# Token-tile pairs of the MoE second layer as 2x2 blocks with seven products, and a new order of the steps

## The chip, the cores and the metric

The kernel runs on one core of one Trainium2 chip. The metric is the device time of one execution in microseconds (us), median of 3 runs. The engines are named as the profile names them: PE (TensorE matmul), PEld (its weight loads), DVE (VectorE), ACT (ScalarE), POOL (GpSimd), SP (the queue that issues the DMAs).

## The reference, cut to what matters

Three stages follow one another: a pooled attention that makes x (2304 tokens, 512 features), a mixture of 8 experts that all see all tokens, and a last two-layer network. The change is in the second of them:

```python
for e in range(E):                       # E = 8, F = 1024, D = 512
    h = np.maximum(x @ w1[e], 0.0)       # first layer
    ye = h @ w2[e]                       # second layer
    out += P[:, e:e + 1] * ye            # gate of each token and expert
```

## The kernel before

A **unit** `u` is 256 of the 8192 hidden columns (two blocks `f` of 128), so there are 32 units, four to an expert. Units 4 to 31 run in the loop that the change touches; each goes through four **slots** `b` = 0 to 3, one for each batch of 576 tokens. Every matrix is held as a high and a low part, and a product is three matmuls (`PASSES`: high by high, high by low, low by high).

In a slot the **first layer** (`mm1w`) is already done by blocks: seven products `m1` to `m7` of 288 columns each on three PSUM banks a, b and e (pool `h`, four banks), with running sums copied out by ACT (`snap`, L588) and added by DVE (`plus`, L591). ACT then writes the high part of `h` (L579) and DVE the low part (L580). PE's inputs for it, `zz`, are made from `zp` by `z_add` (POOL, L535) and `z_split` (ACT L542, POOL L543), one batch ahead. `zp` itself comes once in a unit: `z_heads` (PE, L506, takes all four banks of pool `y`), `z_out` (ACT L516, then a store by SP) and `z_home` (four loads by SP, L524).

The **second layer** is `tile2`: for a tile of 128 tokens six matmuls of 512 columns (L645) into a bank of pool `y`, which DVE multiplies with the gate and adds to `acc` (`put1`, L663). A unit has 18 tiles, in the slots 4, 5, 4 and 5; those of one slot are worked off in the slot after it, between the seven products (`slotw`).

Around this run `w1_split` (ACT L243, POOL L244) and `load_w2` (ACT L131, POOL L132), which split the weights of the next unit, and `conv_units`, the decoding of weights of the last stage, one DVE instruction to a slot from unit 9 on (L151 to L162).

The order of all instructions is written out by hand (`manual_schedule`): each engine executes its own in the order in which the code issues them, and waits where an operand or a buffer isn't ready.

Of the kernel before, what the change touches and what calls it, by code (L numbers as in the profile page):

```python
# [29 lines left out]
BLK = 384  # L30
# [10 lines left out]
W0 = UE  # L41


@with_exitstack
def tile_kernel(ctx: ExitStack, tc: tile.TileContext, qT, kT, vv, pb, w1c, w2c, wcat64, wg, sv, bv, out):
# [7 lines left out]
    far_p = pool("far", 4, space=bass.MemoryType.DRAM)  # L53
    banks = {}
# [78 lines left out]

    RAWS = [(v, half, f) for v in range(1, U2) for half in (1, 0) for f in range(UF)]
# [9 lines left out]

    def raw_ops(key, q):

        v, half, f = key
        lo, hi, m = raw_parts(raws[key], q)
        ex = wt_p[-1].tile([128, 256], U32, tag="ex", name="ex")
# [12 lines left out]
        yield lambda: V.scalar_tensor_tensor(out=m if v else plain(f)[:, o], in0=m, scalar=2.0 ** 20,  # L162
                                             in1=ex.bitcast(F32), op0=ALU.add, op1=ALU.mult)

# [398 lines left out]
    LEFT = {1: 0, 4: 1, 2: 2, 5: 3, 6: 4, 7: 5, 3: 6}  # L563
# [11 lines left out]
    def h_put(b, f, t, p_):  # L575
        s_ = p_[:, :HB]
        o = (b % 2) * S + t * HB
        hh, hl = (h[:, f, k, o:o + HB] for k in range(2))
        A.activation(out=hh, in_=s_, func=AF.Relu)  # L579
        V.scalar_tensor_tensor(out=hl, in0=s_, scalar=0.0, in1=hh.bitcast(F32), op0=ALU.max, op1=ALU.subtract)  # L580

    def mm1w(u, b):

        p, s_ = {}, {}

        def snap(n):
            s_[n] = wt_p[-1].tile([128, BLK], F32, tag=f"snap{n % 2}", name="snap")[:, :HB]
# [5 lines left out]
        def j1():  # L593
            p["a"], p["b"] = psa("h", "ps_a"), psa("h", "ps_b")
            product(1, u, b, p["a"], True)
            snap(1)
            product(2, u, b, p["b"], True)
            plus(1, "b", "b")
            h_put(b, 1, 0, p["b"])

        def j2():
            p["e"] = psa("h", "ps_e")
            product(6, u, b, p["a"])
            snap(2)
            product(7, u, b, p["e"], True)

        def j3():
            product(5, u, b, p["a"])
            snap(3)
            plus(3, "e", "b")  # L610
            h_put(b, 0, 1, p["b"])

        def j4():
            product(3, u, b, p["a"])
            h_put(b, 1, 1, p["a"])
            product(4, u, b, p["e"])
# [19 lines left out]
    def tile2(ws, h, hc, T, put):  # L636
# [10 lines left out]
        put(T, y, acc[:, T, :])  # L647
# [204 lines left out]
    def made(u, pr, q):  # L852
# [3 lines left out]
        return [lambda t=t: tile2(ws, *cols(t), pr * 9 + t, put1(u))  # L856
# [8 lines left out]

    def slotw(u, b, side):

        todo, jobs = ready[:], mm1w(u, b)
        ready[:] = made(u, b // 2, 2 * (b % 2)) + made(u, b // 2, 2 * (b % 2) + 1)
        for n in range(5):  # L870
            for q_, at_ in ((jobs, n + 0.5), (todo, n)):
                if q_:
                    q_.pop(0)()
                for s in side.get(at_, ()):
                    s()

# [35 lines left out]
    with tc.tile_pool(name="ppf", bufs=1) as ppf_p, tc.tile_pool(name="w1p", bufs=2) as w1_, ExitStack() as whole, ExitStack() as start:  # L912
# [163 lines left out]
        conv = {}  # L1076

        def w2_(u):
            if ("w2", u) not in conv:
                conv["w2", u] = load_w2(u)  # L1080
            next(conv["w2", u], None)

        units = conv_units()

        with tc.manual_schedule():
            first = {(0, 1): [(w2_, W0), (x_split, 0)],
                     (0, 2): [(x_split, 1), (x_add, 2)],
                     (0, 3): [(w2_, W0)],
                     (1, 0): [(z_half, W0, 0), (z_half, W0, 1), (x_split, 2)],
                     (1, 1): [(x_add, 3), (load_w1, W0 + 1)],  # L1090
# [5 lines left out]
            for u in range(W0, U1):  # L1096
                for b in range(B):
                    side, last = {n / 2: [] for n in range(10)}, u == U1 - 1
                    if b + 1 < B:
                        side[0].append((z_split, u, b + 1))  # L1100
                    if b + 2 < B:
                        side[3].append((z_add, u, b + 2))
                    if u == W0 and b == 0:
                        side[3].append((pp_split, ))
                    if u == W0 and b == 2:
                        side[1].append((x_split, 3))
                    if last and b < 2:
                        side[2].append((split_plain, b, 0))
                        side[4].append((split_plain, b, 1))
                    if not last:  # L1110
                        if b == 0:
                            side[0].append((w2_, u + 1))
                            side[1].append((w1_split, u + 1, 0))
                            side[2].append((w1_split, u + 1, 1))
                            side[4].append((w2_, u + 1))
                        if b == 1:
                            side[1.5] += [(z_heads, u + 1), (z_out, 0)]
                            side[1].append((z_out, 1))
                        if b == 2:
                            side[0].append((z_home, u + 1))  # L1120
                        if b == 3:
                            side[0].append((z_add, u + 1, 0))
                            side[2].append((z_split, u + 1, 0))
                            side[4].append((z_add, u + 1, 1))
                            if u + 2 < U1:
                                side[2].append((load_w1, u + 2))
                    if u > U1 // 4 and not last:
                        side[(2, 0, 2, 1)[b]].append((next, units, None))
                    if last and b > 2:
                        side[1] += [(low, ), (raw_load, *RAWS[1])]  # L1130
                        side[2].append((low, ))
                    if last and b > 1:
                        for c in range(NC):
                            side[1 + c].append((flip, b - 2, c))
                    slotw(u, b, {n: [lambda f=f, a=a: f(*a) for f, *a in fs] for n, fs in side.items()})
# [4 lines left out]
        sums.append(wt.tile([128, 512], F32, name="sums"))  # L1140
# [97 lines left out]
```

## Time and profile before

| | |
|---|---|
| median of 3 runs | 1702.03 us (1699.96 to 1704.18) |
| profiled execution, span | 1698.2 us |
| around the span, by the median | 3.8 us |
| PE / DVE / ACT / POOL busy | 99% / 67% / 51% / 52% |

The span runs from the first to the last instruction of the core in one profiled execution. The runs were timed without a profile, and no run's own time belongs to the profiled execution alone; the median less the span stands for what lies around it. Busy shares are averages over stages.

### The profile page before, as it was taken

The page shows a single profiled execution, that of the slowest core. Times are in us where ns is not written, and L with a number is a line of the kernel's source. Part 1 is how long each engine was busy: PE and PEld are TensorE (multiplying, and loading weights), DVE is VectorE, ACT ScalarE, POOL GpSimd, SP SyncE. Part 2 cuts the span into 40 slices and gives each one's busy share as a digit, 9 for nine tenths or more (in the row PEclk, how much of TensorE's full clock was granted, in tenths as well). Part 3 has the DMA queues.
Part 4 walks back from the last instruction along what each step waited for, and adds up shares of the span by engine and source line. Part 5 has one row for each costly group of instructions (what it writes and reads, how often), then busy time and mean ns, then how long its engine had stood idle before and what let it go on. Part 6 is the DMA issues. An engine that isn't in the chain of part 4 may idle for free.

```text
span 1698.2 us, 27249 instructions
## 1 busy us (share of the span) xinstructions
PE 1673.7 (99%) x10075; PEld 1449.8 (85%) x10075; DVE 1139.1 (67%) x2246; ACT 874.3 (51%) x1948; POOL 884.0 (52%) x1070
## 2 busy tenths in 40 slices
PE   6999999999999999999999999999999999999999
PEld 4678888888888888888888888888888999989998
DVE  5656656666666666667666667666667877777763
ACT  3543364454454444454544445445445666666664
POOL 0332375555554555655655555555552855555552
PEclk9999999999999999999999999999999999999999
DMA  9610013223232333322332342222310111111103
GB/s 266 170 26 21 18 48 101 77 75 88 75 98 77 101 97 90 87 75 75 95 93 78 99 109 75 75 75 75 100 38 13 38 40 43 44 38 49 48 16 112
DMA packets 60725, 128.13 MB, mean 75 GB/s; under 512 B 5808, under 2 KB 27312, under 8 KB 60592
## 3 DMA queue, kind: packets, MB, share of 16 engines
q1 hardware_dynamic: 60592, 126.39, 27.1%
q8 instruction: 79, 1.29, 0.3%
q14 instruction: 54, 0.44, 0.1%
HBM read 93.34 MB, written 33.03 MB: 74 GB/s over the span
## 4 chain that ended last, share of the span: by engine, by line
PE 96%; DVE 2%; ACT 1%; DMA 1%; issue 0%; SPq 0%; POOL 0%; ACTq 0%; DVEq 0%
PE ps L645 58%; PE ps_a L572 10%; PE ps L688 9%; PE ps_e L572 5%; PE ps L627 3%; PE ps_b L572 3%; PE ps_z L506 3%; PE ps_a L758 1%; DMA q__116<-qT 1%; PE ps_e L758 1%; PE ps_z L452 0%; PE ps_f L810 0%; PE ps_b L758 0%; PE ps_q L346 0%; PE ps_v L331 0%
## 5 line engine op out<-in xcount | busy, mean ns | idle before, releaser
L645 PE MATMUL ps<-w,h 128*128 128x512 f32 x4296 | 1088.4, 394 | 2.9 <-ACT h L579 1.2
L645 PEld LDWEIGHTS ps<-w,h 128*128 128x128 f32 x4296 | 774.5, 188 | 150.1 <-ACT stage L516 4.8
L663 DVE SCALAR_TENSOR_TENSOR acc<-ps,pm,acc 128x512 f32<-128x512 f32 x504 | 372.2, 744 | 167.9 <-PE ps L645 166.9
L543 POOL TENSOR_TENSOR zz<-zp,zz 128x384 fp32r<-128x384 f32 x112 | 115.7, 1033 | 248.2 <-ACT zz L542 137.3
L588 ACT COPY snap<-ps_a 128x288 f32<-128x288 f32 x336 | 134.3, 400 | 204.6 <-PE ps_a L572 203.0
L535 POOL TENSOR_TENSOR sums<-zp 128x128 f32<-128x128 f32 x224 | 105.0, 469 | 167.3 <-DMA zp<-far 163.0
L580 DVE SCALAR_TENSOR_TENSOR h<-ps_b,h 128x288 fp32r<-128x288 f32 x224 | 102.5, 458 | 106.7 <-ACT h L579 106.7
L579 ACT ACTIVATE h<-ps_b 128x288 fp32r<-128x288 f32 x224 | 92.2, 411 | 147.8 <-DVE ps_b L591 147.8
L543 POOL TENSOR_TENSOR zz<-sums,zz 128x512 fp32r<-128x512 f32 x112 | 145.1, 1296 | 0.0
L802 DVE TENSOR_TENSOR acc<-ps,acc 128x512 f32<-128x512 f32 x126 | 86.1, 687 | 82.2 <-PE ps L645 82.0
L572 PEld LDWEIGHTS ps_a<-xt,zz 128*128 128x128 f32 x672 | 113.3, 188 | 18.8 <-ACT snap L588 0.5
L572 PEld LDWEIGHTS ps_a<-xa,zz 128*128 128x128 f32 x672 | 113.1, 188 | 18.0
L680 POOL TENSOR_TENSOR h<-gt,h 128x384 fp32r<-128x384 f32 x64 | 65.9, 1029 | 120.0 <-ACT h L679 110.6
L572 PE MATMUL ps_a<-xt,zz 128*128 128x288 f32 x672 | 125.9, 296 | 0.1
L572 PE MATMUL ps_e<-xt,zz 128*128 128x288 f32 x672 | 125.7, 296 | 0.0
L572 PE MATMUL ps_a<-xa,zz 128*128 128x288 f32 x672 | 125.7, 296 | 0.0
L579 ACT ACTIVATE h<-ps_e 128x288 fp32r<-128x288 f32 x112 | 46.1, 411 | 140.1 <-DVE ps_e L591 140.1
L688 PE MATMUL ps<-xa,w 128*128 128x384 f32 x432 | 110.4, 336 | 0.0
L688 PE MATMUL ps<-xt,w 128*128 128x384 f32 x432 | 110.1, 335 | 0.0
L572 PEld LDWEIGHTS ps_e<-xt,zz 128*128 128x128 f32 x672 | 101.9, 188 | 0.0
L132 POOL TENSOR_TENSOR w<-raw,w 128x1024 fp32r<-128x1024 f32 x31 | 74.5, 2405 | 27.0 <-ACT w L131 26.5
L580 DVE SCALAR_TENSOR_TENSOR h<-ps_e,h 128x288 fp32r<-128x288 f32 x112 | 51.2, 458 | 53.0 <-ACT h L579 53.0
(263 smaller groups left out, 2394.8 us busy)
## 6 DMA issues: line engine op xcount, KB each, us to landing
far<-stage SPq DMA_DIRECT2D x54, 512.0 KB, 2.9
zp<-far SPq DMA_DIRECT2D x108, 256.0 KB, 4.9
raw<-w2c SPq DMA_DIRECT2D x32, 512.0 KB, 7.6
raw<-wcat SPq DMA_DIRECT2D x32, 512.0 KB, 3.8
acc<-kT SPq DMA_DIRECT2D x8, 576.0 KB, 9.4
out<-acc SPq DMA_DIRECT2D x18, 256.0 KB, 2.0
acc<-vv SPq DMA_DIRECT2D x5, 576.0 KB, 10.5
q__114<-qT SPq DMA_DIRECT2D x1, 576.0 KB, 11.6
```

The costliest lines, as they stand in the source:

```text
L132: eng.tensor_tensor(out=w[:, 1, :], in0=r, in1=w[:, 0, :].bitcast(F32), op=ALU.subtract)
L535: G.tensor_tensor(out=sums[:, n], in0=x_, in1=y_, op=op)
L543: G.tensor_tensor(out=zz[:, 1, o], in0=s_, in1=zz[:, 0, o].bitcast(F32), op=ALU.subtract)
L572: mmul(p_[:, :HB], zq_[u, b][:, a, LEFT[n], :], x_, start=start and m == 0, stop=m == 2, skip_group_check=True)
L579: A.activation(out=hh, in_=s_, func=AF.Relu)
L580: V.scalar_tensor_tensor(out=hl, in0=s_, scalar=0.0, in1=hh.bitcast(F32), op0=ALU.max, op1=ALU.subtract)
L588: A.copy(s_[n], p["a"][:, :HB])
L645: mmul(y, h[:, f, a, hc:hc + 128], ws[f][k], start=(n == 0), stop=(n == 3 * UF - 1))
L663: V.scalar_tensor_tensor(out=a, in0=y, scalar=pm[:, T, u // UE:u // UE + 1], in1=a, op0=ALU.mult, op1=ALU.add)
L680: G.tensor_tensor(out=hl, in0=g, in1=hh.bitcast(F32), op=ALU.subtract)
L688: mmul(p, w[:, a, c * 128:(c + 1) * 128], x_get(k, c, b), start=(n == 0), stop=(n == 3 * NC - 1))
L802: V.tensor_tensor(out=a, in0=y, in1=a, op=ALU.add)
```

## The change

In units 5 to 30 (26 units) two pairs of token tiles, one at the end of batch 1 and one at the start of batch 2, leave `tile2`. Their 256 tokens by 256 hidden columns are taken as a 2x2 block matrix, as is `w2` (256 by 512), and multiplied with seven products `p1` to `p7` of three 256-column matmuls each (`set7`), in two banks of pool `y` (`a2`, and `b2` whose halves are b and e). Batch 1's set runs in slot 2, batch 2's in slot 3. It needs sums of the blocks of `h` (`h_plain` ACT, `h_sums` DVE, `h_split` ACT and POOL) and of `w2` (`t_add` POOL, `t_split` ACT and POOL), five additions into `acc` by DVE (`d1`, `d2`, `d3`, `d4`, `d7`) and two by ACT and POOL together (`k5`, `k6`). The low part of `w1_split` goes from POOL to DVE. `z_add` has the same four additions, to other places, and `z_split` three pieces in place of two. The decoded weights of the last stage wait in DRAM instead of SBUF (`send`, `plain_home`). In these units the order of a slot's steps is a string of tokens: `m` first-layer product, `n` snap, `+` plus, `r`/`l` high/low part of `h`, `t` tile, `te` its put, `x` a put left from the slot before, `p`/`d`/`k` the set, `zh`/`zo`/`zs`/`za` the z steps, `hs` `h_split`, `S` `h_sums`, `cv` one decoding step, `wl`/`w2s` loading and splitting w2, `w1l`/`w1a`/`w1b` the same of w1, `ta`/`ts` `t_add` and `t_split`.

The diff, cut to its core; `mm1w` is only taken apart into the tokens, and unit 4 and unit 31 keep the old order (`PLAIN`).

```diff
+SEVEN = (1, 2)
+def by7(u, b):
+    return W0 < u < U1 - 1 and b in SEVEN
...
+    raw2, w_t = {}, {}
+    def w2_load(u):
+        raw2[u] = raw_p.tile([128, 1024], F32, tag="raw", name="raw")
+        nc.sync.dma_start(out=raw2[u], in_=w2c[u])
+    def w2_split(u):
+        w = w_new((2, u))
+        split(w, raw2[u])
+    def t_add(u):
+        b11, b12, b21, b22 = (raw2[u][:, 256 * n:256 * n + 256] for n in range(4))
+        for to, x_, y_ in ((b11, b12, b11), (b12, b22, b12), (b22, b22, b11), (b21, b21, b22)):
+            G.tensor_tensor(out=to, in0=x_, in1=y_, op=ALU.subtract)
+    def t_split(u):
+        w_t[u] = w_p.tile([128, 2, 1024], F32R, tag="w", name="w_t")
+        split(w_t[u], raw2.pop(u))
...
+        ex = stay[0][:, :256].bitcast(U32) if stay else wt_p[-1].tile([128, 256], U32, tag="ex", name="ex")
...
+        if not v:
+            yield lambda: send(f, o, ex)
+    def send(f, o, ex):
+        if f not in ready_far:
+            ready_far[f] = far0_p.tile([128, 1024], F32, tag=f"conv{f}", name="conv")
+        nc.sync.dma_start(out=ready_far[f][:, o], in_=ex.bitcast(F32))
...
-        split(w1s[u][:, :, o], wts[1, u][:, o])
+        split(w1s[u][:, :, o], wts[1, u][:, o], V)
...
+        two = stay[0][:, 256:].rearrange("p (n m) -> p n m", n=2)
+        one = wt_p[-1].tile([128, 1, 128], F32, tag="sums", name="sums")
+        for to, x_, y_, op in ((two[:, 0], src[:, 0], src[:, 2], ALU.add),
+                               (two[:, 1], two[:, 0], src[:, 1], ALU.subtract),
+                               (one[:, 0], src[:, 1], src[:, 0], ALU.subtract),
+                               (src[:, 0], src[:, 3], two[:, 1], ALU.subtract)):
+            G.tensor_tensor(out=to, in0=x_, in1=y_, op=op)
+        z_sums[u, b] = [(slice(0, 4), src), (slice(4, 6), two), (slice(6, 7), one)]
...
+    hp = {}
+    def h_plain(b, f, p_):
+        if f == 1 - b % 2:
+            hp[b] = wt_p[-1].tile([128, UF, 2, 128], F32, tag="hp", bufs=2, name="hp")
+        o = HB - 256 if b % 2 else 0
+        A.activation(out=hp[b][:, f].rearrange("p t m -> p (t m)"), in_=p_[:, o:o + 256], func=AF.Relu)
+    def h_mixed(b):
+        rows = [x_[:, 0, :].rearrange("p (r t) -> p r t", r=4) for x_ in xa]
+        return [x_[:, 2 * (b % 2):2 * (b % 2) + 2, HB:HB + 256] for x_ in rows]
+    def h_sums(b):
+        a11, a21, a12, a22 = (hp[b][:, f, t] for f in range(2) for t in range(2))
+        for to, x_, y_, op in ((a22, a21, a22, ALU.add), (a21, a11, a21, ALU.subtract),
+                               (a11, a22, a11, ALU.subtract), (a12, a12, a11, ALU.subtract)):
+            V.tensor_tensor(out=to, in0=x_, in1=y_, op=op)
+    def h_split(b):
+        from_ = hp[b].rearrange("p f t m -> p f (t m)")
+        hi, lo = h_mixed(b)
+        A.copy(hi, from_)
+        G.tensor_tensor(out=lo, in0=from_, in1=hi.bitcast(F32), op=ALU.subtract)
+    def set7(u, b):
+        e_, t0 = u // UE, 7 * (b % 2)
+        w2, wt, p = wts[2, u], w_t[u], {}
+        kept_ = hp[b].rearrange("p f t m -> p f (t m)")
+        parts = {1: ((0, 0), w2, 0), 2: ((1, 0), w2, 2), 4: ((1, 1), wt, 2), 3: ((1, 0), w2, 3),
+                 5: ((1, 1), wt, 0), 6: ((0, 0), wt, 3), 7: ((0, 1), wt, 1)}
+        def product(n, to, start=False):
+            (f, t), w, part = parts[n]
+            for m, (a, k) in enumerate(PASSES):
+                if n in (1, 2, 4):
+                    o = (t0 + t) * 128
+                    l_ = h[:, f, a, o:o + 128]
+                else:
+                    l_ = h_mixed(b)[a][:, f, 128 * t:128 * t + 128]
+                mmul(to, l_, w[:, k, 256 * part:256 * part + 256], start=start and m == 0, stop=m == 2,
+                     skip_group_check=True)
+        def place(t, d):
+            T = 9 * (b // 2) + t0 + t
+            return acc[:, T, 256 * d:256 * d + 256], pm[:, T, e_:e_ + 1]
+        def add(t, d, from_):
+            a, g = place(t, d)
+            V.scalar_tensor_tensor(out=a, in0=from_, scalar=g, in1=a, op0=ALU.mult, op1=ALU.add)
+        def snap(d):
+            a, g = place(1, d)
+            A.activation(out=kept_[:, d], in_=p["a"], func=AF.Copy, scale=g)
+            G.tensor_tensor(out=a, in0=a, in1=kept_[:, d], op=ALU.add)
+        def p1():
+            p["a"] = psa("y", "ps_a2")[:, :256]
+            product(1, p["a"], True)
+        def p2():
+            b_ = psa("y", "ps_b2")
+            p["b"], p["e"] = b_[:, :256], b_[:, 256:]
+            product(2, p["b"], True)
+        jobs = {"p1": p1, "p2": p2, "p7": lambda: product(7, p["e"], True),
+                "k6": lambda: snap(0), "k5": lambda: snap(1)}
+        for n, to in ((6, "a"), (5, "a"), (3, "a"), (4, "e")):
+            jobs[f"p{n}"] = lambda n=n, to=to: product(n, p[to])
+        for n, t, d, bank in ((1, 0, 0, "a"), (2, 0, 0, "b"), (7, 1, 1, "e"), (4, 1, 0, "e"), (3, 0, 1, "a")):
+            jobs[f"d{n}"] = lambda t=t, d=d, bank=bank: add(t, d, p[bank])
+        return jobs
...
+    def h_high(u, b, f, t, p_):
+        if by7(u, b) and t == b % 2:
+            h_plain(b, f, p_)
+        A.activation(out=h_at(b, f, t)[0], in_=p_[:, :HB], func=AF.Relu)
...
+    PLAIN = ("m1 n1 m2 +b x x rb lb .5 t te 0 m6 n2 m7 1.5 t te 1 m5 n3 +c rc lc 2.5 t te 2 m3 ra la m4 +e re le S 3.5"
+             " t te 3 4.5 t te 4")
+    STEADY = {
+        0: "m1 x m2 n1 +b rb t m6 lb m7 n2 x t te te zs m5 n3 +c w1a rc cv t lc w1b m3 m4 ra te +e t te la re le ta t za ts te",
+        1: "m2 m1 m7 cv t n1 zs +b m6 te rb lb n2 zh zo0 t te m5 zo1 n3 t +c rc te m3 ra za lc m4 +e re la le t zs3 te S",
+        2: "x p1 wl m1 n1 m2 +b hs rb t d1 home m6 te n2 t lb x p2 d2 p6 k6 te m5 n3 p7 m7 p5 d7 k5 m3 ra +c p4 rc cv m4 la +e re lc d4 p3 za le d3 t S",
+        3: "m1 m2 n1 +b hs rb p1 x m6 t lb n2 d1 p2 zs cv m7 p6 k6 m5 d2 n3 x +c p7 d7 p5 k5 m3 t rc ra m4 lc la p4 +e za w2s re d4 p3 le te d3 w1l",
+    }
+    seven, left = {}, []
...
+        if "set" in seven:
+            of = seven.pop("set")()
+            jobs |= of | {"d3": lambda: left.append(of["d3"])}
+        if by7(u, b):
+            seven["set"] = lambda: set7(u, b)
+            ready[:] = ready[:3] if b % 2 else ready[2:]
...
+        def steady(u, b):
+            jobs = ({"zs": (z_split, u, 1), "w1a": (w1_split, u + 1, 0), "w1b": (w1_split, u + 1, 1),
+                     "za": (z_add, u, 2), "ta": (t_add, u), "ts": (t_split, u)},
+                    {"zs": (z_split, u, 2), "zh": (z_heads, u + 1), "zo0": (z_out, 0), "zo1": (z_out, 1),
+                     "za": (z_add, u, 3), "zs3": (z_split, u, 3)},
+                    {"home": (z_home, u + 1), "wl": (w2_load, u + 1), "za": (z_add, u + 1, 0)},
+                    {"zs": (z_split, u + 1, 0), "za": (z_add, u + 1, 1), "w2s": (w2_split, u + 1)})[b]
+            if b == 3 and u + 2 < U1:
+                jobs["w1l"] = load_w1, u + 2
+            if by7(u, b - 1) and b:
+                jobs["hs"] = h_split, b - 1
+            if u > U1 // 4:
+                jobs["cv"] = next, units, None
+            return jobs
...
+                        if u == U1 - 2 and b == 3:
+                            at("w2s", plain_home)
```

## Rows read from the trace of the kernel before

**Rows 1.** The page: span, and busy time of each engine.

```profile
span 1698.2 us, 27249 instructions
PE 1673.7 (99%) x10075; PEld 1449.8 (85%) x10075; DVE 1139.1 (67%) x2246; ACT 874.3 (51%) x1948; POOL 884.0 (52%) x1070
```

**Rows 2.** The page: the chain that ended last, by line.

```profile
PE ps L645 58%; PE ps_a L572 10%; PE ps L688 9%; PE ps_e L572 5%; PE ps L627 3%; PE ps_b L572 3%; PE ps_z L506 3%; PE ps_a L758 1%; DMA q__116<-qT 1%; PE ps_e L758 1%; PE ps_z L452 0%; PE ps_f L810 0%; PE ps_b L758 0%; PE ps_q L346 0%; PE ps_v L331 0%
```

**Rows 3.** The chain, one unit: start, length, what, matmuls.

```profile
845.47 1.69 PE ps_z L506 x24
847.16 1.59 PE ps L645 x6
...
859.64 2.75 PE ps L645 x12
...
868.92 0.40 PE ps_e L572 x3
```

**Rows 4.** Windows, the same unit: length, busy time (instructions) of each engine.

```profile
845.40:883.30 37.90, 37.90 (x219) 32.98 (x218) 25.57 (x51) 18.75 (x44) 21.07 (x28) 1.00 0.32 84
```

**Rows 5.** The chain, last stage: matmuls of 384 columns.

```profile
1347.68 4.18 PE ps L688 x24
```

**Rows 6.** Groups by form, whole span: transposes on PE (count, busy us, mean ns).

```profile
L250 PE MATMUL ps_w<-ident 128*128 128x128 f32 x38 | 4.4, 274 | 0.0
```

**Rows 7.** Groups by form, whole span: DVE.

```profile
L663 DVE SCALAR_TENSOR_TENSOR acc<-ps,pm,acc 128x512 f32<-128x512 f32 x504 | 372.2, 744 | 167.9 <-PE ps L645 166.9
L591 DVE TENSOR_TENSOR ps_b<-ps_b,snap 128x288 f32<-128x288 f32 x112 | 51.4, 459 | 6.6 <-ACT snap L588 4.0
L463 DVE TENSOR_TENSOR z<-ps_z,z 128x256 fp32r<-128x256 f32 x16 | 5.8, 418 | 0.3 <-ACT z L462 0.3
L431 DVE TENSOR_TENSOR pm<-pm,skr 128x144 f32<-128x144 f32 x8 | 2.4, 304 | 0.2
L376 DVE TENSOR_TENSOR xa<-a2T,xa 128x576 fp32r<-128x576 f32 x3 | 2.3, 759 | 2.2 <-ACT xa L375 2.2
```

**Rows 8.** Groups by form, whole span: ACT and POOL.

```profile
L542 ACT CAST zz<-sums 128x512 fp32r<-128x512 f32 x112 | 69.7, 622 | 0.0
L462 ACT CAST z<-ps_z 128x256 fp32r<-128x256 f32 x16 | 4.9, 386 | 0.4 <-PE ps_z L452 0.4
L579 ACT ACTIVATE h<-ps_b 128x288 fp32r<-128x288 f32 x224 | 92.2, 411 | 147.8 <-DVE ps_b L591 147.8
L543 POOL TENSOR_TENSOR zz<-sums,zz 128x512 fp32r<-128x512 f32 x112 | 145.1, 1296 | 0.0
L207 POOL TENSOR_TENSOR sums<-sums,w 128x256 f32<-128x256 f32 x24 | 18.0, 751 | 1.9
L535 POOL TENSOR_TENSOR sums<-zp 128x128 f32<-128x128 f32 x224 | 105.0, 469 | 167.3 <-DMA zp<-far 163.0
L132 POOL TENSOR_TENSOR w<-raw,w 128x1024 fp32r<-128x1024 f32 x31 | 74.5, 2405 | 27.0 <-ACT w L131 26.5
```

**Rows 9.** Timeline: two decoding steps of DVE, with POOL beside one.

```profile
801.65 1.29 POOL L244 TENSOR_TENSOR w1s<-w__8681,w1s 128x512 fp32r<-128x512 f32 x1 [0.40 <-ACT w1s L243]
802.13 0.96 DVE L154 TENSOR_SCALAR ex<-ex 128x256 uint32<-128x256 uint32 x1
...
867.45 0.28 DVE L153 TENSOR_SCALAR ex<-ex 128x256 uint32<-128x256 uint32 x1
```

**Rows 10.** Groups by form, 512 to 1249 us: two of the decoding steps.

```profile
L158 DVE TENSOR_SCALAR raw<-raw 128x256 uint32<-128x256 uint32 x9 | 5.5, 608 | 0.0
...
L154 DVE TENSOR_SCALAR ex<-ex 128x256 uint32<-128x256 uint32 x9 | 4.0, 444 | 0.0
```

**Rows 11.** Timeline: two puts of DVE back to back.

```profile
861.84 1.40 DVE L663 SCALAR_TENSOR_TENSOR acc<-ps,pm,acc 128x512 f32<-128x512 f32 x2
```

**Rows 12.** Timeline: loads of `z_home`, and the first `z_add` behind them.

```profile
856.40 1.74 SPq L524 DMA_DIRECT2D zp<-far  x4
...
863.73 0.46 POOL L535 TENSOR_TENSOR sums<-zp 128x128 f32<-128x128 f32 x1 [6.11 <-DMA zp<-far]
```

More of the change, by code (lines that the diff above doesn't have):

```diff
@@ L53, in tile_kernel @@
     far_p = pool("far", 4, space=bass.MemoryType.DRAM)
+    far0_p = pool("far0", 1, space=bass.MemoryType.DRAM)
     banks = {}
@@ L143, in raw_parts @@
         return rv[:, :, 0], rv[:, :, 1], rv[:, :, 0].bitcast(F32)
+    stay, ready_far = [], {}
     def raw_ops(key, q):
@@ L161, in raw_ops @@
             lows.append(((3, v, f), o, m))
[L162 removed]
+        yield lambda: V.scalar_tensor_tensor(out=m if v else ex.bitcast(F32), in0=m, scalar=2.0 ** 20,
                                              in1=ex.bitcast(F32), op0=ALU.add, op1=ALU.mult)
+        if not v:
[4 more added lines that the diff above has]
+        nc.sync.dma_start(out=ready_far[f][:, o], in_=ex.bitcast(F32))
     def low():
@@ L230, in plain, with plain_home @@
     def plain(f):
-        if not w_plain:
-            w_plain.append(w_p.tile([128, 2, 1024], F32, tag="w", name="w_plain"))
         return w_plain[0][:, f]
+    def plain_home():
+        w_plain.append(w_p.tile([128, 2, 1024], F32, tag="w", name="w_plain"))
+        for f in range(UF):
+            nc.sync.dma_start(out=plain(f), in_=ready_far[f])
     def split_plain(f, half):
@@ L582, in mm1w, with h_at, h_low @@
+    def h_at(b, f, t):
+        o = (b % 2) * S + t * HB
+        return [h[:, f, k, o:o + HB] for k in range(2)]
+    def h_high(u, b, f, t, p_):
+        if by7(u, b) and t == b % 2:
+            h_plain(b, f, p_)
+        A.activation(out=h_at(b, f, t)[0], in_=p_[:, :HB], func=AF.Relu)
+    def h_low(b, f, t, p_):
+        hh, hl = h_at(b, f, t)
+        V.scalar_tensor_tensor(out=hl, in0=p_[:, :HB], scalar=0.0, in1=hh.bitcast(F32), op0=ALU.max, op1=ALU.subtract)
     def mm1w(u, b):
@@ L586, in snap @@
         def snap(n):
-            s_[n] = wt_p[-1].tile([128, BLK], F32, tag=f"snap{n % 2}", name="snap")[:, :HB]
+            s_[n] = wt_p[-1].tile([128, HB], F32, tag=f"snap{n % 2}", name="snap")
             A.copy(s_[n], p["a"][:, :HB])
@@ L634, in tile_kernel, with tile2 @@
     to_gate, no_gate = [], []
-    def tile2(ws, h, hc, T, put):
+    def tile2(ws, h, hc, T, put, later=None):
         if not no_gate:
@@ L646, in tile2 @@
                 n += 1
-        put(T, y, acc[:, T, :])
+        out_ = lambda: put(T, y, acc[:, T, :])
+        if later is None:
+            out_()
+        else:
+            later.append(out_)
     def gated(T):
@@ L864, in slot1, with run @@
         slot(first, side, 0 if u < UP and (u, q) != (0, 2) else 1)
+    PLAIN = ("m1 n1 m2 +b x x rb lb .5 t te 0 m6 n2 m7 1.5 t te 1 m5 n3 +c rc lc 2.5 t te 2 m3 ra la m4 +e re le S 3.5"
+             " t te 3 4.5 t te 4")
+    STEADY = {
[4 rows of a table added]
+    }
+    seven, left = {}, []
     def slotw(u, b, side):
-        todo, jobs = ready[:], mm1w(u, b)
+        todo, later, late, jobs = ready[:], [], left[:], mm1w(u, b)
+        del left[:]
         ready[:] = made(u, b // 2, 2 * (b % 2)) + made(u, b // 2, 2 * (b % 2) + 1)
[L870 to L874, printed above, removed]
-                    s()
+        if "set" in seven:
[4 more added lines that the diff above has]
+            ready[:] = ready[:3] if b % 2 else ready[2:]
+        def run(token):
+            if token in jobs:
+                jobs[token]()
+            elif token == "t":
+                if todo:
+                    todo.pop(0)(later)
+            elif token in ("te", "x"):
+                if (later, late)[token == "x"]:
+                    (later, late)[token == "x"].pop(0)()
+            elif token[0] not in "pdk":
+                for s in side.get(token, ()):
+                    s()
+        steady = W0 < u < U1 - 1
+        for token in (STEADY[b] if steady else PLAIN).split():
+            run(token)
+        left[:0] = late + later
+        assert not todo
     def tiles2(v, b):
@@ L1097, in tile_kernel @@
                 for b in range(B):
[L1098 to L1118, printed above, removed]
-                        if b == 2:
[L1120 to L1135, printed above, removed]
+                    last, side = u == U1 - 1, {}
@@ new lines, in at @@
+                    def at(place, f, *a):
+                        side.setdefault(place, []).append(lambda: f(*a))
+                    if u == W0 or last:
+                        if b + 1 < B:
+                            at("0", z_split, u, b + 1)
+                        if b + 2 < B:
+                            at("3", z_add, u, b + 2)
+                        if last and b < 2:
+                            at("2", split_plain, b, 0)
+                            at("4", split_plain, b, 1)
+                        if last and b > 2:
+                            at("1", low)
+                            at("1", raw_load, *RAWS[1])
+                            at("2", low)
+                        if last and b > 1:
+                            for c in range(NC):
+                                at(str(1 + c), flip, b - 2, c)
@@ new lines, in tile_kernel @@
+                    if u == W0:
+                        if b == 2:
+                            at("1", x_split, 3)
+                        for place, what in {0: {"1": "w1a", "2": "w1b"}, 1: {"1.5": "zh zo0", "1": "zo1"},
+                                            2: {"0": "home wl", "3": "za"},
+                                            3: {"1.5": "zs", "2": "w1l", "3.5": "za", "4": "w2s"}}[b].items():
+                            for token in what.split():
+                                at(place, *steady(u, b)[token])
+                    elif not last:
+                        for token, job in steady(u, b).items():
+                            at(token, *job)
+                        if u == U1 - 2 and b == 3:
+                            at("w2s", plain_home)
@@ L1136, in tile_kernel @@
+                    slotw(u, b, side)
         zt += [z_p.tile([128, 2048], F32R, tag="z", name="zt") for _ in range(3)]
@@ L1139, in tile_kernel @@
         gt.append(ppf_p.tile([128, B, 128], F32, name="ppf", tag="ppf").rearrange("p b m -> p (b m)")[:, :BLK])
-        sums.append(wt.tile([128, 512], F32, name="sums"))
+        for f in left:
+            f()
+        of_moe.close()
+        stay.clear()
+        wt_p.append(whole.enter_context(tc.tile_pool(name="m2", bufs=1)))
+        sums.append(wt_p[-1].tile([128, 512], F32, name="sums"))
         todo, count = ready[:], 0
```

72 lines of the change are left out of this document (29 added, 43 removed).

## Prediction, before the changed kernel was run

> **What bounds the kernel now.** I read the page first: PE is busy 99% of the span [rows 1], and the chain that ended last is PE on 96 of 100 parts, L645 alone on 58 [rows 2]. That is busy time of a pipelined engine, so I next read the chain of a single unit, which lists PE's work piece by piece with hardly a gap [rows 3]. A unit is 28 first-layer products of 0.40 us, 18 tiles of 1.375 us (2.75 us for two) and 1.69 us of z_heads: 11.2 + 24.8 + 1.7 = 37.7 us, against 37.90 us in the windows [rows 4]. The missing 0.2 us is the step from z_heads back to a tile (1.59 us for that tile's piece). So PE is not merely busy, it is at its pace, and nothing else ends last in this stage. DVE, ACT and POOL work 25.6, 18.8 and 21.1 us of the 37.9 [rows 4]. A change gains here only what it takes from PE's columns, and loses whatever makes PE wait.
>
> **PE's side.** A pair of tiles costs 12 matmuls, 2.75 us [rows 3]. In its place stand 21 matmuls of 256 columns. No full-height matmul of that width is in the trace. Its pace follows from two neighbours: 384 columns take 4.18/24 = 0.174 us [rows 5], 288 take 0.398/3 = 0.133 us [rows 3], so 0.43 ns a column, and 256 columns come to 0.119 us. z_heads, with 256 columns in pairs of half-height matmuls, has 1.69/12 = 0.14 us a pair with its ramp, which does not contradict it. Bounds: 0.133 if a matmul this short waits for its weights, and (4.4 - 0.27)/37 = 0.112 us, the pace of the 128-column transposes [rows 6]. I take 0.119, an interpolation a third of a step outside two close rows. Then a set costs 21 x 0.119 = 2.50 us and saves 0.25; two sets in 26 units save 52 x 0.25 = 13.0 us. The ends are 2.79 us (a loss of 2 us in all) and 2.35 us (a gain of 21 us).
>
> **Work on the other engines, per unit.**
> DVE loses four puts of 0.744 and gains ten additions of 128x256 (between 0.418, the same size without a gate, and 0.744, twice the size with one [rows 7]; near the first, 0.47), eight sums of 128x128 and two low halves of w1, 128x512. The last two read both operands from SBUF; by L431 and L376, which do so too, they cost 0.29 and 0.69 us [rows 7]. That makes 25.6 - 3.0 + 4.7 + 2.3 + 1.4 = 31.0 us.
> POOL loses the two w1 halves (2 x 1.30) and gains t_add (4 x 0.75), the low half of t_split (2.41), two of h_split (2 x 1.30), four halves of k5 and k6 (4 x 0.75) and 0.2 us in each z_split: 21.1 - 2.6 + 3.0 + 2.4 + 2.6 + 3.0 + 0.8 = 30.3 us [rows 4, 8].
> ACT gains h_plain and k5, k6 (8 x 0.39), h_split (2 x 0.62), t_split (about 1.1 by the step from 256 to 512 columns) and 0.7 for z_split's third piece: 24.9 us [rows 4, 8].
> All stay under a new unit of 37.4 us, at 83%, 81% and 67%. So no engine replaces PE by its sum; what counts is the order. These costs are nothing only while the three chains below meet PE in time.
>
> **Chain 1, the sums of h in slot 2.** At the end of slot 1 the last tile's put (0.74) stands in DVE's queue before h_sums, so the sums begin about 0.85 us into slot 2. Four of 0.29, ACT's copy (0.62 for 128x512) and POOL's low half (1.30) follow, with some 0.15 for handing over: 4.1 us. PE needs the low half in p6's third matmul, after p1, m1, m2, a tile, m6, a tile, p2 and two of p6: 3 x 0.40 + 2 x 1.375 + 2 x 0.36 + 0.24 = 4.9 us. So 0.8 us is in hand if nothing interferes. But POOL is then busy with the three pieces of zs3 (from about 0.4 us on), and the trace shows what that does: L153 took 0.28 us alone, its like L154 0.96 us when it came into a POOL instruction, ending 0.15 us after it [rows 9]. Over the steady stage such steps took 0.61 and 0.44 us in the mean, 0.32 and 0.16 longer than 0.28 [rows 10]. At a mean of 0.24 each, the four sums lose 1.0 us and the chain ends at 5.1: 0.1 us too late at most, and I charge 0.1. If each sum waits for a whole piece of zs3 (1.30, 0.75, 0.47), the last ends near 3.5 us and the low half near 5.5: 0.6 us too late. [...]
> In slot 3 the sums follow the low part of h directly, without a put before them, and p6 comes 3.9 us into the slot; the same sum leaves the same reserve.
>
> **Chain 2, DVE through slot 0.** Slot 0 now has five tiles' puts and w1's low halves on DVE. From m5's snap on, DVE owes +c, w1a, cv, lc, w1b, te, +e, te and la before bank a is free for m7 of slot 1: 0.46 + 0.69 + 0.42 + 0.46 + 0.69 + 0.74 + 0.46 + 0.74 + 0.46 = 5.1 us, less 8 x 0.08 because neighbours overlap (two puts of 0.744 in 1.40 us [rows 11]): 4.5 us. PE needs three tiles and four products to get there, 5.7 us, less 0.45 until the snap is out: 5.3. Of the 0.8 in hand, w1a, cv and w1b lose 3 x 0.24. In time with 0.1 to spare; I charge 0.05 for what scatters past it.
>
> **Chain 3, the loads of zp.** They move from slot 2's start behind zs3's reading of zp, that is behind POOL's first piece, 1.7 us into slot 2; SP's queue has only the load of w2 before them, and the w1 load after. From the first issue to the first z_add took 863.73 - 856.40 = 7.3 us [rows 12]. So z_add runs from 9.0 to 10.9 us, POOL's low half for slot 3 to about 12.5, and p6's third matmul there is at 9.4 + 3.9 = 13.3 us. 0.8 in hand. The cover is the whole of slot 2: a load 2 us later would cost 1.2 us in each unit.
>
> The other waits are shorter. p7 shares its bank with d2: between p2's end and p7 lie p6 and m5, 0.76 us, against d2's 0.47. The set keeps two of the four y banks, and each tile's put comes before the next but one tile. d3 is put off to slots 3 and 0, so its bank is late; the tile that takes the bank comes over 1 us after it. The decoded weights' trip over DRAM is eight stores and two loads of 512 KB, long before their use. Moving w1's, w2's and z's splits earlier or later by half a slot changes no product that waits for them today.
>
> **Sum.** -13.0 + 26 x (0.1 + 0.05) = -9.1 us. On the profiled execution 1698.2 - 9.1 = 1689.1 us span; with the 3.8 us around it, which is the median of the runs less the span, 1693 us.
>
> **The rivals.**
> *The shared access eats the gain (same).* Each sum of chain 1 waits for a whole POOL piece: 0.6 us in 26 units is 16 us, so 1702 - 13 + 16 = 1705. For it: the sums start exactly inside zs3, and DVE and POOL took turns in every such meeting that I looked at. Against: the mean delay is well under that.
> *z_heads waits for DVE (slower).* In slot 1 DVE's cv stands before +b and the first tile's put, and that put frees the fourth y bank, which z_heads needs about 4 us into the slot. If cv comes after t_split's low half has begun (2.41 us on POOL, after zs, t_add and z_add, 7.4 us of POOL work that starts with slot 0's second half), it is held until some 4.3 us into slot 1, and the put ends at 5.5: z_heads loses 1.5 us. 70 of the 88 cv places hold a decoding step, so about 18 units pay: 27 us, 1702 - 13 + 27 = 1716 us. It decides from 13/18 = 0.7 us on. For it: by my count cv and the start of that half are within 0.7 us of each other. Against: any delay of POOL puts cv first.
> *Another pace.* At 0.133 us the products save nothing: 1704. At 0.112: 1681.
>
> **Chances.** My forecast 0.55 (its own range 1688 to 1697), the first rival 0.17, the second 0.23, slow pace 0.02, fast pace 0.03. Changes under 0.3%, 5 us, can hardly be told from none. Faster: 0.55 + 0.03 = 0.58; same: 0.17 + 0.02 = 0.19; slower 0.23. For 8 in 10 the range runs from 1687, a little under the full gain without any wait, to 1718, the second rival whole.
>
> **What the changed profile would show.** Right: 256-column matmuls at 0.119 us, a unit of about 37.5 us, DVE near 31 and POOL near 30 us in it, PE without a gap before p6's third matmul. Wrong: idle time of PE before p6 put down to POOL's h_split (chain 1 or 3), before m7 or z_heads put down to DVE (chain 2, second rival), w1's low halves on DVE well over 0.69 us, or sets of 2.8 us.

## The result and the profile after

The changed kernel is slower: 1726.42 us in the median (1724.53 to 1726.79), against 1700.99 us for the kernel before in the four runs made beside it, a ratio of 1.0146 (95% interval 1.0132 to 1.0161). The forecast was 1693 us, with a range to 1718. The profiled execution has a span of 1722.8 us, 24.6 us more than before.

The page of the changed kernel: span, busy time of each engine, and the chain that ended last by engine and by line (what [rows 1, 2] show of before):

```profile
span 1722.8 us, 29594 instructions
PE 1677.8 (97%) x10543; PEld 1469.4 (85%) x10543; DVE 1303.7 (76%) x2664; ACT 998.6 (58%) x2346; POOL 1136.6 (66%) x1414
PE 75%; DVE 14%; POOL 4%; ACT 4%; issue 2%; DMA 0%; SPq 0%; ACTq 0%; DVEq 0%; POOLq 0%
PE ps L768 37%; PE ps L815 9%; PE ps_a L616 7%; PE ps_e L616 4%; PE ps_a L663 4%; DVE acc L790 4%; DVE hp L638 4%; PE ps_b L663 3%; PE ps L750 2%; PE ps_z L547 2%; DVE h L707 2%; POOL xa L645 2%; DVE w1s L285 2%; PE ps_a L885 1%; PE ps_b L616 1%
```

Lines have moved: the products of `mm1w` are now at L616, those of the sets at L663, the tiles at L768, the sums of `h` at L638, the low half of `h_split` at L645, w1's low halves at L285. Read the last two lines first. The chain was PE on 96 of 100 parts in the kernel before:

```profile
PE 96%; DVE 2%; ACT 1%; DMA 1%; issue 0%; SPq 0%; POOL 0%; ACTq 0%; DVEq 0%
```

Now PE has 75, DVE 14 and POOL 4, and three of the new lines stand in it: L638, L645 and L285. PE is still 97% busy, and that is the trap of such a page: PE needs only a few hundredths of idle time for 25 us to go.

The windows of two units, from one z_heads to the next, which answer to [rows 4] (length; busy time and instructions of PE, PEld, DVE, ACT, POOL):

```profile
821.79:860.90 39.11, 38.20 (x236) 33.57 (x235) 32.09 (x66) 23.36 (x60) 30.93 (x41) 1.00 0.33 85
860.90:900.00 39.10, 38.12 (x237) 33.64 (x236) 32.58 (x67) 23.35 (x60) 30.93 (x41) 1.00 0.33 82
```

These units take 39.1 us instead of 37.9, and PE is idle for 0.9 us of each, where before it was idle for none. The view of waits says for what (engine, line, who released it: us in total, times, longest); the two lines below have no counterpart before, and no other wait that comes back from unit to unit sums to 1 us:

```profile
PE ps_a L663 <- POOL xa L645: 15.5, 26, 0.6
PE ps_e L616 <- DVE h L707: 5.7, 17, 0.4
```

A wait costs more than its idle time, because a matmul that finds PE empty takes its whole length (0.39 us for 256 columns) instead of the pace (0.12). So I took from the trace, for 25 units and each position in a unit, the distance between the ends of successive matmuls and subtracted the pace. All of it sums to 45.7 us, against 9.6 before. p6's third matmul in slot 2 pays 0.86 us in every unit, 21.5 us; m7 in slot 1 pays 0.57 to 0.65 us in 17 units, 10.2 us; p6, m6 and p5 in slot 3 pay 2.3, 2.0 and 1.7 us in all; the tile behind z_heads pays 7.4 us, 6.5 before. Against these 36 us stand 25 x 0.5 = 12.5 us that the products save. The difference, 23.6 us in 25 units, is nearly the whole of the 24.6 us between the spans.

The chain through slot 2 of a unit (start, length, what), where slot 2 begins with p1 at 828.95:

```profile
829.38 0.66 DVE acc L790
830.04 0.89 DVE hp L638
...
830.96 0.71 DVE hp L638
...
831.69 0.44 DVE hp L638
...
832.16 0.30 DVE hp L638
...
832.54 0.63 ACT xa L644
...
833.24 1.30 POOL xa L645
...
834.58 0.39 PE ps_a L663
...
835.37 0.36 PE ps_b L663 x3
```

and the timeline of POOL and PE beside it (start, length, engine, line, operation; in brackets the idle time before):

```profile
829.48 1.30 POOL L587 TENSOR_TENSOR zz<-zp,zz 128x512 fp32r<-128x512 f32 x1 [1.99 <-ACT zz L586]
830.73 0.78 POOL L587 TENSOR_TENSOR zz<-ppf,zz 128x256 fp32r<-128x256 f32 x1
831.47 0.51 POOL L587 TENSOR_TENSOR zz<-sums,zz 128x128 fp32r<-128x128 f32 x1
...
833.59 0.39 PE L663 MATMUL ps_a<-w_t,xa 128*128 128x256 f32 x2
...
834.58 0.39 PE L663 MATMUL ps_a<-w_t,xa 128*128 128x256 f32 x1 [0.60 <-POOL xa L645]
```

The four sums have the same shape, and take 0.89, 0.71, 0.44 and 0.30 us. Put them beside POOL's three pieces of zs3, which end at 830.78, 831.51 and 831.98: the first three sums end at 830.93, 831.67 and 832.13, each 0.15 us after one of the pieces. The fourth has no piece beside it and takes 0.30. The prediction's own sign of this, "ending 0.15 us after it" [rows 9], is repeated three times in a row. The last line of the chain gives the pace of the new matmuls: 0.36 us for three.

The chain through slot 0 of the same unit, to m7 of slot 1 at 819.40:

```profile
813.71 0.63 ACT w1s L284
...
814.37 0.91 DVE w1s L285
815.27 0.88 DVE raw L188
816.15 0.37 DVE h L707
816.52 0.78 DVE w1s L285
817.30 0.66 DVE acc L790
817.96 0.37 DVE ps_e L718
818.33 0.65 DVE acc L790
818.98 0.38 DVE h L707
...
819.40 0.68 PE ps_e L616 x3
```

It is DVE's queue without a gap: the two low halves of w1 with a decoding step (L188, which reads two operands from SBUF) between them, then two puts, and behind all of it the low part of `h` (L707) that frees bank a. POOL beside it, in the timeline: the last piece of zs, then the first two of t_add's four.

```profile
814.26 0.46 POOL L587 TENSOR_TENSOR zz<-sums,zz 128x128 fp32r<-128x128 f32 x1
814.69 1.19 POOL L154 TENSOR_TENSOR raw<-raw 128x256 f32<-128x256 f32 x1
...
815.95 0.80 POOL L154 TENSOR_TENSOR raw<-raw 128x256 f32<-128x256 f32 x1
```

The sums' pattern comes back: these pieces end at 814.72, 815.88 and 816.75, and the first half, the decoding step and the second half end 0.55, 0.27 and 0.55 us behind them, in turn. And the groups by form over the whole span, which answer to [rows 7, 8] (busy us, mean ns of one):

```profile
L638 DVE TENSOR_TENSOR hp<-hp 128x128 f32<-128x128 f32 x208 | 100.5, 483 | 5.4
L285 DVE TENSOR_TENSOR w1s<-w__9623,w1s 128x512 fp32r<-128x512 f32 x2 | 1.8, 881 | 0.1
L154 POOL TENSOR_TENSOR raw<-raw 128x256 f32<-128x256 f32 x104 | 97.6, 938 | 6.1
```

The sums were put at 0.29 us and take 0.483; w1's low halves at 0.69 and take 0.88 here (most units between 0.88 and 0.92); POOL's t_add was put at 0.75 and takes 0.938, so the delay seems to go both ways (e4 below settles it).

### The profile page after: what moved, and what is told of

The parts are those of the page before. It is cut to its first block, busy times and chain, and to the rows that moved or that the text cites. A ratio compares the mean times of both kernels' runs of the same rounds, so it can differ in the third digit from the quotient of the medians.

```text
span 1722.8 us, 29594 instructions
## 1 busy us (share of the span) xinstructions
PE 1677.8 (97%) x10543; PEld 1469.4 (85%) x10543; DVE 1303.7 (76%) x2664; ACT 998.6 (58%) x2346; POOL 1136.6 (66%) x1414
## 4 chain that ended last, share of the span: by engine, by line
PE 75%; DVE 14%; POOL 4%; ACT 4%; issue 2%; DMA 0%; SPq 0%; ACTq 0%; DVEq 0%; POOLq 0%
PE ps L768 37%; PE ps L815 9%; PE ps_a L616 7%; PE ps_e L616 4%; PE ps_a L663 4%; DVE acc L790 4%; DVE hp L638 4%; PE ps_b L663 3%; PE ps L750 2%; PE ps_z L547 2%; DVE h L707 2%; POOL xa L645 2%; DVE w1s L285 2%; PE ps_a L885 1%; PE ps_b L616 1%
## 5 line engine op out<-in xcount | busy, mean ns | idle before, releaser
L768 PE MATMUL ps<-w,h 128*128 128x512 f32 x3672 | 930.4, 394 | 3.4 <-ACT h L703 1.9
L768 PEld LDWEIGHTS ps<-w,h 128*128 128x128 f32 x3672 | 662.5, 188 | 128.7 <-ACT stage L557 6.1
L790 DVE SCALAR_TENSOR_TENSOR acc<-ps,pm,acc 128x512 f32<-128x512 f32 x400 | 295.0, 743 | 98.0 <-PE ps L768 97.7
L587 POOL TENSOR_TENSOR zz<-zp,zz 128x512 fp32r<-128x512 f32 x112 | 146.9, 1312 | 72.1 <-ACT zz L586 71.6
L616 PE MATMUL ps_e<-xt,zz 128*128 128x288 f32 x672 | 127.7, 298 | 5.8 <-DVE h L707 5.7
L616 PE MATMUL ps_a<-xt,zz 128*128 128x288 f32 x672 | 127.7, 299 | 0.1
L707 DVE SCALAR_TENSOR_TENSOR h<-ps_b,h 128x288 fp32r<-128x288 f32 x224 | 101.3, 452 | 33.0 <-ACT h L703 32.4
L616 PE MATMUL ps_a<-xa,zz 128*128 128x288 f32 x672 | 125.9, 296 | 0.0
L616 PEld LDWEIGHTS ps_a<-xt,zz 128*128 128x128 f32 x672 | 108.0, 188 | 12.5 <-ACT snap L715 0.7
L645 POOL TENSOR_TENSOR xa<-hp,xa 128x512 fp32r<-128x512 f32 x52 | 67.3, 1294 | 69.8 <-ACT xa L644 69.8
L616 PEld LDWEIGHTS ps_e<-xt,zz 128*128 128x128 f32 x672 | 101.9, 189 | 12.2 <-DVE h L707 9.6
L616 PEld LDWEIGHTS ps_a<-xa,zz 128*128 128x128 f32 x672 | 105.1, 188 | 7.4 <-POOL zz L587 0.3
L677 POOL TENSOR_TENSOR acc<-acc,hp 128x256 f32<-128x256 f32 x104 | 75.9, 740 | 46.6 <-ACT hp L676 40.5
L638 DVE TENSOR_TENSOR hp<-hp 128x128 f32<-128x128 f32 x208 | 100.5, 483 | 5.4
L154 POOL TENSOR_TENSOR raw<-raw 128x256 f32<-128x256 f32 x104 | 97.6, 938 | 6.1
```

The costliest lines, as they stand in the source:

```text
L154: G.tensor_tensor(out=to, in0=x_, in1=y_, op=ALU.subtract)
L587: G.tensor_tensor(out=zz[:, 1, o], in0=s_, in1=zz[:, 0, o].bitcast(F32), op=ALU.subtract)
L616: mmul(p_[:, :HB], zq_[u, b][:, a, LEFT[n], :], x_, start=start and m == 0, stop=m == 2, skip_group_check=True)
L638: V.tensor_tensor(out=to, in0=x_, in1=y_, op=op)
L645: G.tensor_tensor(out=lo, in0=from_, in1=hi.bitcast(F32), op=ALU.subtract)
L707: V.scalar_tensor_tensor(out=hl, in0=p_[:, :HB], scalar=0.0, in1=hh.bitcast(F32), op0=ALU.max, op1=ALU.subtract)
```

## The experiments

Two theories at first. A: the sums of `h` wait in turn for POOL's pieces (each ended 0.15 us after one, above), and their lateness is p6's wait. B: the chain is late for another reason (the put ahead of the sums, or the length of ACT's and POOL's parts), and the sums' length hardly matters. C is A's counterpart for slot 0: bank a is freed too late because of what stands before `la` (the low part of `h` from bank a) in DVE's queue.

**e1: one operand of the sums from PSUM.** Seven of eight sums take the plain value from the bank in which PE left it and apply the relu on the way, so that they read one operand from SBUF (the times below are followed by their ratio to the kernel before, with its 95% interval):

```diff
-    def h_sums(b):
+    def h_sums(b, p):
...
+        def relu(to, from_, y_, op):
+            V.scalar_tensor_tensor(out=to, in0=from_, scalar=0.0, in1=y_, op0=ALU.max, op1=op)
...
+            relu(a22, ps(right_, 1), a21, ALU.add)
+        relu(a21, ps(left_, 0), a21, ALU.subtract)
+        relu(a11, ps(left_, 0), a22, ALU.subtract)
...
+            relu(a12, ps(right_, 0), a11, ALU.add)
```

> The sums of h read one operand from PSUM (the other sign of one sum is taken up in the sums of w2), so that seven of the eight have a single SBUF operand; they stand in the same place, behind the same put, and the whole result is computed. Theory A (DVE and POOL exclude each other when both read SBUF, so each sum waits for a piece of zs3): the four sums of slot 2 take 1.2 us instead of 2.5, p6's third matmul no longer waits 0.86 us, and 26 units give back 22 us: 1704 us. Theory B (the chain is late because the sums stand behind the last tile's put): the start is the same, so 1726 us within 4.

Some signs of the sums differ by this, and `t_add` follows. In this run one of its block sums carries the other sign in the wrong block, so the values of p4 and p6 are not the reference's, against what the expectation says; no instruction, size or order hangs on that, and f1, with the sign in its own block, keeps the gain. Measured: 1704.76 us, 1.0028 (1.0019 to 1.0038). 21.7 us of the 25.4 are gone with no instruction taken out. Groups by form of e1, the sums with a PSUM operand, and the one that still has two in SBUF:

```profile
L641 DVE SCALAR_TENSOR_TENSOR hp<-ps_e,hp 128x128 f32<-128x128 f32 x78 | 17.6, 280 | 0.0
...
L641 DVE SCALAR_TENSOR_TENSOR hp<-ps_b,hp 128x128 f32<-128x128 f32 x52 | 12.7, 286 | 0.9
L652 DVE TENSOR_TENSOR hp<-hp 128x128 f32<-128x128 f32 x26 | 9.5, 366 | 0.9
```

and its waits of PE:

```profile
PE ps_e L616 <- DVE h L721: 5.6, 17, 0.4
...
PE ps_a L677 <- POOL xa L659: 1.8, 3, 0.7
```

p6's wait falls from 15.5 us to 1.8 (three times, in slot 3); m7's stays as it was. A holds for sums with both operands in SBUF (the sums of e1 still read one there, and take 280 to 286 ns); B doesn't.

**g1: the same instruction, both operands in SBUF.** e1 changed the kind of instruction as well. This run changes only that:

```diff
-            V.tensor_tensor(out=to, in0=x_, in1=y_, op=op)
+            V.scalar_tensor_tensor(out=to, in0=x_, scalar=0.0, in1=y_, op0=ALU.max, op1=op)
```

> A control for the first experiment: the sums of h are the same kind of instruction as there (the first operand clipped at zero, which changes no value), but with both operands in SBUF as in the changed kernel. Theory A: place of the operands decides, the sums take 0.48 us in the mean and the time stays at 1726 us. Rival F (the kind of instruction decides): 0.28 us and 1704 us.

Measured: 1727.86 us, 1.0164 (1.0149 to 1.0179): nothing gained. Its sums by form, and its wait of PE:

```profile
L638 DVE SCALAR_TENSOR_TENSOR hp<-hp 128x128 f32<-128x128 f32 x208 | 102.0, 490 | 5.4
PE ps_a L663 <- POOL xa L645: 15.5, 26, 0.6
```

490 ns against 280 to 286 for the same instruction: it is where the operands lie.

**e2: the sums ahead of the last put and of zs3.**

```diff
-... re la le t zs3 te S"
+... re la le S t zs3 te"
```

> The sums of slot 1 stand before the last tile's put instead of behind it, nothing else. Theory B: they begin 0.66 us earlier and p6's third matmul waits 0.2 us instead of 0.86: 17 us less, 1709 us. Theory A: they still meet the three pieces of zs3 on POOL, the last sum ends with the last piece as before: 0 to 8 us less, most likely 3: 1723 us.

Measured: 1726.48 us, 1.015 (1.0135 to 1.0165), no gain, nearer A than B. The mean of a sum even grows:

```profile
L638 DVE TENSOR_TENSOR hp<-hp 128x128 f32<-128x128 f32 x208 | 110.6, 532 | 5.4
```

p6's third matmul loses only 0.36 us instead of 0.86, but now p6's first loses 0.18 and p7 0.24, 0.78 in all. The last sum again ends 0.15 us after POOL's last piece, whose place has not changed, 3.17 us into slot 2 instead of 3.50: only 0.33 of the 0.66 us are left. And the put that stood ahead of the sums now stands behind them, with d1 behind it; d1 ends 4.59 us into the slot instead of 4.26. Starting the sums earlier did not help here, where POOL's pieces set their end.

**e3: `la` before two puts in slot 0.**

```diff
-... m3 m4 ra te +e t te la re le ta ...
+... m3 m4 ra la te +e t te re le ta ...
```

> In slot 0 the low part of the bank-a result of the first layer (la) moves up, ahead of the put, +e and the next put, nothing else. Theory C (m7 of slot 1 waits 0.58 us in two of three units for la, which DVE reaches late): the wait goes, 10 us less: 1716 us. Rival D (DVE is too full in slot 0, whatever the order): the wait moves to the next bank that DVE has to free, 1726 us within 4.

Measured: 1715.87 us, 1.0092 (1.0077 to 1.0107), 10.6 us less than the changed kernel; of the two waits only one is left in the view of waits:

```profile
PE ps_a L663 <- POOL xa L645: 15.4, 26, 0.6
```

C holds, and by the size of the wait that was counted.

**e4: w1's low halves back on POOL.**

```diff
-        split(w1s[u][:, :, o], wts[1, u][:, o], V)
+        split(w1s[u][:, :, o], wts[1, u][:, o])
```

> The low halves of w1 go back from DVE to POOL, one part of the change undone. Theory C and D both: DVE has 1.4 us and two waits for POOL less in slot 0, so m7's wait in slot 1 goes, 10 us less: 1716 us, if POOL's 2.6 us more in slot 0 stay hidden. If POOL is what is short, its later pieces come late instead and the time stays at 1726 or grows.

Measured: 1761.56 us, 1.036 (1.0345 to 1.0376), 35 us more than the changed kernel: the 1716 us is a miss, and what came is the other branch, that POOL is short. Its waits of PE:

```profile
PE ps_a L616 <- ACT snap L715: 29.7, 26, 1.4
...
PE ps L768 <- ACT stage L557: 12.3, 26, 0.5
```

m7's wait is gone, as C said, but m6 of slot 1 waits for ACT, which is busy for only 23.23 of 39.00 us (window 800:839). The timeline at one such place:

```profile
794.30 2.55 POOL L285 TENSOR_TENSOR w1s<-w__9150,w1s 128x512 fp32r<-128x512 f32 x2
...
796.81 3.18 POOL L154 TENSOR_TENSOR raw<-raw 128x256 f32<-128x256 f32 x4
...
800.03 1.04 ACT L284 CAST w_t<-raw 128x1024 fp32r<-128x1024 f32 x1 [3.79 <-POOL raw L154]
...
800.98 0.39 ACT L715 COPY snap<-ps_a 128x288 f32<-128x288 f32 x1
...
801.43 0.66 PE L616 MATMUL ps_a<-xt,zz 128*128 128x288 f32 x3 [1.10 <-ACT snap L715]
```

POOL works off the two halves (2.55 us) before t_add; ACT's copy for t_split stands in its queue, waits 3.79 us for it, and behind it stands the snap that frees bank a for m6. In this unit the late POOL stopped PE for 1.10 us, through the queue of a third engine. The run also settles POOL's side: with the halves off DVE, the four additions of t_add take 3.18 us in the unit shown, where they take 3.96 to 4.04 us in every unit of the changed kernel (4.03 from 814.69).

**f1: e1 and e3 together**, with the sign in its own block.

> The two undone waits together: the sums of h read one operand from PSUM (as in the first experiment, with the opposite sign carried by the fourth block's sum of w2, so that the whole result is computed), and la stands early in slot 0. If the two waits are separate (theories A and C), their gains add: 1704.8 less 10.5 is 1694 us, 0.4% below the kernel before. If freeing one only lets the other wait begin elsewhere, the sum is less: 1700 or more.

Measured: 1695.39 us in the median of 12 runs, 0.9972 (0.9962 to 0.9982): faster than both kernels. The interval lies below 1, though 0.28% is just under the 0.3% that the prediction called distinguishable. The first line of the page of f1:

```profile
span 1693.1 us, 29594 instructions
```

and the window of one of its units:

```profile
776.00:813.70 37.70, 37.69 (x236) 33.44 (x235) 30.84 (x67) 23.23 (x58) 30.81 (x41) 1.00 0.31 80
```

The unit has 37.70 us and PE no gap to speak of. The instructions are as many as in the changed kernel (29594). Most units take 37.60 to 37.75 us; the same count by position gives 18.0 us over 25 units, 8.4 above before: 1.4 more behind z_heads, 2.5 at p7, 1.9, 1.7 and 1.6 at p5, m6 and p6 of slot 3; the rest cancels to within 1 us. 12.5 - 8.4 = 4.1 us, near the 5.1 between the spans.

**f2: m7 ahead of p7 in f1.**

```diff
-... n3 p7 m7 p5 d7 k5 ...
+... n3 m7 p7 p5 d7 k5 ...
```

> The same with m7 ahead of p7 in slot 2, so that d2 has 0.4 us more to free the bank that p7 writes. The 0.10 us that p7 waits in each of 26 units go: 2.6 us below the kernel with both, 1692 us. If d2 isn't what p7 waits for, no difference.

Measured: 1696.38 us, 0.9973 (0.9962 to 0.9983), the same as f1, but not because d2 isn't what p7 waits for. p7's 0.10 us in each unit goes, and p4, which waits for p7's result to be taken, loses 0.09 instead. The timeline of f1 shows why the 0.10 is there at all:

```profile
779.31 0.48 DVE L687 SCALAR_TENSOR_TENSOR acc<-ps_b,pm,acc 128x256 f32<-128x256 f32 x1 [0.92 <-PE ps_b L678]
779.85 0.62 PE L678 MATMUL ps_b<-w_t,xa 128*128 128x256 f32 x3
```

DVE was free (0.92 us idle) and d2 starts as soon as p2 is done; its 0.48 us and the handing over are what p7 waits for.

**e5: the new order without products** (`SEVEN = ()`, plain tiles in the places of the sets; t_add and t_split still made).

> No sets: all 18 tiles of a unit go through the old product, in the new order with the tiles in the places of the sets; the sums of h fall away, those of w2 are still formed and not used. Theory A and C: the 13 us of the products are lost and the 22 us of p6's wait with them, m7's wait stays: 1726 + 13 - 22 = 1717 us. Rival E (the new order costs nothing of its own, all loss comes with the sets): 1702 us.

Measured: 1734.4 us, 1.0203 (1.0189 to 1.0216), neither value. Of the changed kernel's waits hardly any is left (m7 loses 0.06 us), but three came with the places that I gave the tiles: the first tile of slot 0 loses 0.48 us, m6 of slot 3 0.42, the tile behind z_heads 0.71 instead of 0.28. It says nothing of the order by itself; what the order alone costs stays open.

## Why the prediction was wrong

**PE's side was right.** 0.119 us was interpolated, 0.36/3 = 0.12 is in the chain, 118 ns is the median distance of two such matmuls. A set costs 2.5 us, and f1, where the two large waits are gone, shows the gain less the 8.4 us of small ones.

**Chain 1 failed, by the size of one term.** Its clock was near: sums from 0.85 us (1.09 measured), ACT 0.62, POOL 1.30, PE there at 4.9 (5.0). The step that failed is "At a mean of 0.24 each, the four sums lose 1.0 us", which puts their end at 0.85 + 1.2 + 1.0 = 3.0 us into the slot. They take 2.4 us and end at 3.5. The later start is not the reason: e2 starts them 0.66 us earlier and gains 0.33 of it, because POOL's last piece sets the end. The full-blocking end, "the low half near 5.5: 0.6 us too late", is what happened (5.59, and 0.60 idle). The mean over a stage [rows 10] was the wrong price here: it averages steps that meet POOL and steps that don't, while these four run one after the other beside three pieces of POOL. And the 0.6 was priced at 0.6, but cost 0.86, as PE starts again with a whole matmul. 26 x 0.86 = 22.4 us where the sum had 2.6.

The first rival therefore describes what happened to the sums (0.89, 0.71 and 0.44 us beside POOL's three pieces), and its 1705 us would have been 1711 with the true price; the second loss, 10.6 us in 26 units, takes it nearly all the way to 1726.

**Chain 2 failed likewise, smaller.** In the unit shown the first w1 half, cv and the second half take 0.91, 0.96 and 0.86 us by the timeline (the chain counts each to the start of the next: 0.91, 0.88, 0.78), where 0.69, 0.42 and 0.69 were put: 0.93 us more, against the 3 x 0.24 = 0.72 charged. With a little less overlap, DVE is done 5.5 us after the snap (819.36 - 813.81) instead of 4.5 + 0.7 = 5.2, and PE is there after 5.2 us (819.40 less 0.37 of idle time) instead of 5.3. So the "0.1 to spare" became 0.37 us of idle time, 0.6 us of cost, in all the units where cv is a decoding step, 17 of 25. In the other 8, where nothing is decoded there, m7 waits for nothing, though the halves take 0.91 and 0.86 us there too: that is the switch. That POOL lengthens cv and the halves is read from the three pieces shown above, which they follow in turn; no run shortened them where they stand, and e3 took the wait away by order alone.

**The evidence for the price.** The sums take 483 ns (the changed kernel) and 490 ns (g1) with two operands in SBUF, and 280 to 286 with one (e1). The decoding steps of [rows 9] are of another kind: L153 and L154 read a single tensor, and L154 was held all the same (0.96 us against 0.28). The prediction had two prices, a whole piece of POOL for each sum, which was its estimate from the lengths of the pieces, and the mean of [rows 10], and took the mean; the whole piece, applied to each sum, gave 0.6 us.

**The rest.** Chain 3 was in time nearly always: loads at 830.80, first z_add at 838.54, 7.7 us for 7.3. In slot 3, where the prediction gave the sums the same reserve, p6 lost 2.3 us in 25 units. The second rival, z_heads waiting for DVE, did not occur: from the matmul before it to its first end 0.31 us pass, as before, so its forecast of a slower kernel was not what came. p7 against d2, called 0.76 for 0.47, was tighter than that: once p6 no longer waits, p7 loses 0.10 (f1). The engines' sums were near (DVE 32.1 for 31, POOL 30.9 for 30), and said nothing, as the prediction held: "what counts is the order".

## What to carry to other kernels

When DVE gets work with two SBUF operands, look for what POOL does in the same microseconds, instruction by instruction, and price each as held until POOL's piece ends, as three of the four sums were here (0.89, 0.71 and 0.44 us instead of 0.30); a mean over a stage hides it. If one operand is still in PSUM, try reading it from there: in e1 that gave back 22 us without removing an instruction. And a chain that by the sum ends within 0.1 us of when PE needs it is not safely in time: both such chains here came late. Price a wait at its idle time plus what the next matmul takes beyond its pace when it starts on an empty engine (0.39 - 0.12 us here).

## What the runs showed of the hardware

In the changed kernel the sums of `h`, which read two operands from SBUF, and POOL's pieces took turns at instruction boundaries: the row of short sums beside the row of POOL instructions ran at the pace of the POOL pieces (sums of 0.30 us took 0.89, 0.71 and 0.44 beside pieces of 1.30, 0.78 and 0.51, each ending 0.15 us after one). With one operand in PSUM and the other still in SBUF the sums took 0.28 to 0.29 us in the mean beside the same pieces (in f1 one of 0.29 us from 776.31, inside a piece of 0.73 from 776.25). Reading a single operand was not enough by itself: the decoding steps with one operand, all of it SBUF, were held too (0.83 us for L183 in slot 0, at 619.68 and 697.96 of the changed kernel, against 0.28 for its like alone in [rows 9]). POOL paid as well: the four additions of t_add took 3.96 to 4.04 us in a unit with w1's halves on DVE and 3.18 in the unit shown without (e4), so moving these halves from POOL to DVE lengthened what was left on POOL; still, e4, which moved them back, was the slowest of all, at 1761.56 us. And the sum of an engine's busy time did not tell the time in any of these runs: in the units shown DVE, ACT and POOL all stayed under 84%.
